# Layer B's projections of queries and keys: ScalarE reads a bank three times before VectorE's lower part

## The chip, the cores and the metric

The kernel runs on one core of one Trainium2 chip. The metric is device time in microseconds of one execution of the whole program (four layers). Five engines work in parallel, each through its own list of instructions in order: TensorE (PE, matrix products; PEld are its weight loads), VectorE (DVE), ScalarE (ACT), GpSimd (POOL) and SyncE (SP), which here issues most of the transfers. They wait for each other by semaphores. Matrix products land in PSUM, which the kernel uses as eight banks of 128 x 512 fp32 ("ps").

## The reference

Four layers run one after the other on a sequence of 2048 tokens of width 640, with 32 heads of width 20: A, B, A, B, each with a layer norm ahead and a residual sum behind.

```
x = x + A(layernorm(x)); x = x + B(layernorm(x)); x = x + A(...); x = x + B(...)

A: q, k, v = heads of x @ wqkv;  phi(t) = (t+1 if t > 0 else exp(t)) + 1e-6
   kv = sum_s phi(k) v^T;  z = sum_s phi(k)
   out = (phi(q) kv / (phi(q) z + 1e-6)) @ wo

B: q, k, v = x @ wq, x @ wk, x @ wv, cut into heads and 4 segments of 512 tokens
   phi(t) = t+1 if t > 0 else exp(t);  g = sigmoid(beta), one per head;  M = z = 0
   for each segment s:
       a_dot = softmax(q_s k_s^T / sqrt(20) + causal mask) v_s
       a_mem = phi(q_s) M / (phi(q_s) z + 1e-6)
       o_s   = g * a_mem + (1 - g) * a_dot
       M += phi(k_s) v_s^T;  z += sum phi(k_s)
   out = concat(o) @ wo
```

So the projected q and k of layer B are used twice: in the softmax attention of their own segment, and through phi in the memory. The first segment has no memory to read (M = 0), so its q needs no phi; the last has nobody to write a memory for, so its k needs none.

## The kernel before, in words

Numbers that need more than fp16 are carried as a sum of two fp16 tensors, an upper and a lower part. The weights and the normalized, transposed input are split like that, and a projection `proj_t` (L380 to L394) makes one bank of 128 output columns x 512 tokens from 15 matrix products of 512 columns (five blocks of 128 input columns, three products each).

Layer B's `b_project` (L867) handles a segment of 512 tokens: first v, then for each of the five blocks t of 128 columns q and then k. For each of these banks p:

- `split_store` (L853) takes the upper fp16 part with ScalarE (L857) and, from p and the upper part, the lower one with VectorE (L858), into a buffer `nat` (two of them). Then two transfers by SP's queue write both to memory, L861 and L862 for q, L864 and L865 for k.
- where phi is needed, `phi` (L419) makes e = exp(p) (L423) and r = relu(p) (L425) on ScalarE, both into a pool `er` of three buffers, and VectorE puts them together, min(e, 1) + r (L430), as `pq` for q or `pkT` for k. The bank is free when its last reader is done.

Of the 40 banks in one run of layer B, the 15 of q in segments 1 to 3 and the 15 of k in segments 0 to 2 have phi; the 5 of q in segment 0 and the 5 of k in segment 3 are split only. The layer runs twice, so 60 of 80 banks have phi. From pkT, TensorE makes a transpose (L885), ScalarE copies it (`pkt`, L887), and products with v (L893) are added to the memory `acc` by VectorE (L898, L900).

The attention of a segment (`attention`, L1106) starts when the segment's projections are done, and so runs beside the projections of the next segment. It works on 8 groups of four heads, in three stretches of steps each, with groups pipelined: row maxima (`row_max`: products L1008, VectorE's masked maximum L1015), the maxima as extra rows of q (`split_max` L1024, `max_rows`: transpose L1033, ScalarE's copy `mt` L1035, SP's transfer L1038), scores and exponentials (`scores`: products L1050, ScalarE's exponential `pe` L1054, GpSimd's causal mask L1061), the weighted sum with v (`weigh`, L1077), a copy (L1083), a transpose and the normalization (L1090 to L1101; `tmp` of L1100 comes from the pool `er` too). The stacks of q and k are loaded from memory by SP (L994).

Before that, layer A's end (`a_second`) and behind it the output projection of B (`b_out`) run as further streams; both transpose their input through a bank, which ScalarE (L329) and VectorE (L330) split into an upper and a lower part, called `oT`, for products at L401.

Two generators, one for the dense work and one for attention, are stepped by their estimated TensorE costs. TensorE's order is the order of the program text as these streams give it. The other engines' lists are ordered by the framework's scheduler from the dependencies, with the program order as priority. The framework also puts the wait for an earlier reader of a PSUM bank on another engine's next reader: in the kernel before, ScalarE's e waits for VectorE's lower part of the same bank.

Of the kernel before, what the change touches and what calls it, by code (L numbers as in the profile page):

```python
# [11 lines left out]
BF16 = mybir.dt.bfloat16  # L12
# [9 lines left out]
P = 128  # L22
C = D // P
SEG = 512
NSEG = S // SEG
# [102 lines left out]
def pause(n):  # L128
    for _ in range(n):
        yield 0.0  # L130
# [12 lines left out]
class Kernel:  # L143
# [272 lines left out]
        nc.vector.scalar_tensor_tensor(e, e, 1.0, r, op0=OP.min, op1=OP.add)  # L416
        return e

    def phi(self, p, inv, dst, eps):  # L419
        nc, sb = self.nc, self.sb  # L420
        n = p.shape[-1]
        e = sb.tile([P, 512], F32, tag="er", name="e", bufs=3)[:, :n]
        nc.scalar.activation(e, p, AF.Exp, scale=inv)  # L423
        r = sb.tile([P, 512], F32, tag="er", name="r", bufs=3)[:, :n]
        nc.scalar.activation(r, p, AF.Relu, scale=inv)  # L425
        if eps:
            nc.gpsimd.tensor_scalar(e, e, 1.0, eps, op0=OP.min, op1=OP.add)  # L427
            nc.vector.tensor_tensor(dst, e, r, op=OP.add)
        else:
            nc.vector.scalar_tensor_tensor(dst, e, 1.0, r, op0=OP.min, op1=OP.add)  # L430
# [419 lines left out]
            for a in (60, 124):  # L850
                nc.sync.dma_start(k[a:a + 2], one[:2])

    def split_store(self, p, dd, t, key):  # L853

        nc = self.nc
        nat = self.bp.tile([P, 2, SEG], F16, tag="nat", name="nat", bufs=2)
        nc.scalar.activation(nat[:, 0], p, AF.Copy, scale=QK_SHIFT)  # L857
        nc.vector.scalar_tensor_tensor(nat[:, 1], p, QK_SHIFT, nat[:, 0], op0=OP.mult, op1=OP.subtract)  # L858
        d = dd[t * P:(t + 1) * P]
        if key == "q":  # L860
            self.q_nat.dma_start(d[:, 0:3:2], nat)  # L861
            self.q_nat.dma_start(d[:, 1], nat[:, 0])  # L862
        else:
            self.q_nat.dma_start(d[:, 0:2], nat)  # L864
            self.q_nat.dma_start(d[:, 2], nat[:, 0])  # L865

    def b_project(self, st):  # L867

        nc, sb, bp = self.nc, self.sb, self.bp
        s, w, xT, acc = st["s"], st["w"], st["xT"], st["acc"]  # L870
        st["qd"] = self.dr.tile([D, 3, SEG], F16, tag="qd", name="qd", bufs=2)
        st["kd"] = self.dr.tile([D, 3, SEG], F16, tag="kd", name="kd", bufs=2)
        if "before" in st:
            yield lambda: st["before"].get("attended")
        for i in range(NT):
            st["v"].append(self.new_v(st))
            for n in range(2):
                self.v_half(self.proj_n(xT, w["v"], i, n), st["v"][i], n)
                yield self.COST_N
        pkT = pk = None  # L880

        def pk_turn():
            pt = self.bank()
            for i in range(NT):
                nc.tensor.transpose(pt[:, i * P:(i + 1) * P], pkT[:, i * P:(i + 1) * P], self.ident)  # L885
            pk = bp.tile([P, SEG], F32, tag="pkt", name="pkt", bufs=1)
            nc.scalar.activation(pk, pt, AF.Copy)  # L887
            return pk

        def update(t, pk):  # L890
            pm = self.bank()
            for i in range(NT):
                nc.tensor.matmul(pm[:, :WID[t]], pk[:, i * P:(i + 1) * P],  # L893
                                 st["v"][i][:, LO[t] * E1:LO[t] * E1 + WID[t]],
                                 start=i == 0, stop=i == NT - 1)
            a = acc[:, OFF[t]:OFF[t] + WID[t]]
            if s == 0:
                nc.vector.tensor_copy(a, pm[:, :WID[t]])  # L898
            else:
                nc.vector.tensor_tensor(a, pm[:, :WID[t]], a, op=OP.add)  # L900

        for t in range(C):
            p = yield from self.proj_t(xT, w["q"], t)
            self.split_store(p, st["qd"], t, "q")
            if s > 0:
                pq = sb.tile([P, SEG], F32, tag="pq", name="pq", bufs=PQ)
                self.phi(p, self.inv["B", "q"], pq, 0)
                st["pq"].append(pq)
            yield self.COST_T
            st["half"] = t >= 2  # L910
            if pkT is not None:
                pk = pk_turn()
                yield 440
            p = yield from self.proj_t(xT, w["k"], t)
            self.split_store(p, st["kd"], t, "k")
            if s < NSEG - 1:
                pkT = bp.tile([P, SEG], F32, tag="pkT", name="pkT", bufs=1)
                self.phi(p, self.inv["B", "k"], pkT, 0)
            yield self.COST_T
            if pk is not None:  # L920
                update(t - 1, pk)
                yield 4 * 4 * WID[t - 1] * COL
        st["projected"] = True

        def rest():
            if s == 0:
                yield from pause(4)
            if s < NSEG - 1:
                pk = pk_turn()
                yield 440  # L930
                update(C - 1, pk)
                yield 4 * 4 * WID[C - 1] * COL
                st["mem"] = self.masked(acc, self.gblk)
        st["rest"] = rest()
# [64 lines left out]
    def row_max(self, G, todo):  # L999

        nc, bp, qs, ks = self.nc, self.bp, G["qs"], G["ks"]
        bs = [self.bank() for _ in range(2)]
        cost = 0
        for p, i, a in todo:
            n = (i + 1) * P
            for par in range(2):
                r = slice(64 * par, 64 * par + 60)
                nc.tensor.matmul(bs[par][:, a:a + n], qs[r, p, i * P:(i + 1) * P], ks[r, p, :n],  # L1008
                                 start=True, stop=True)
                cost += n * COL  # L1010
        for par in range(2):
            for p, i, a in todo:
                n = (i + 1) * P
                junk = bp.tile([P, SEG], BF16, tag="junk", name="junk", bufs=1)
                nc.vector.tensor_tensor_reduce(bs[par][:, a:a + n], bs[par][:, a:a + n], self.maskw[:, SEG - n:],  # L1015
                                               1.0, NEG, OP.add, OP.max, G["mg"][:, par, p, i:i + 1])
        return cost
# [347 lines left out]
```

## Time and profile before

| | us |
|---|---|
| median of three runs | 1744.88 |
| lowest and highest | 1742.05, 1745.94 |
| the profiled execution | 1743.11 |
| its span in the trace | 1741.4 |

| engine | busy in the span |
|---|---|
| PE | 1668.7 us, 96% |
| DVE | 1183.8 us, 68% |
| PEld | 1048.4 us, 60% |
| ACT | 969.3 us, 56% |
| POOL | 518.7 us, 30% |

The mean granted TensorE clock of the execution is 0.998 of full speed. A line of the profile that names a group reads: source line, engine, operation, what it writes <- what it reads with shape and type, count, then busy time in us and mean ns of one, then the idle time of the engine ahead of these instructions and what ended most of it. A row of the timeline reads: start in us, duration, engine, line, operation, tiles, count of instructions joined in the row, and in brackets the engine's idle time just before with what released it. The chain that ended last is followed back from the last instruction, at each step to what released it.

### The profile page before, as it was taken

To read this page: it belongs to the slowest core of one execution; us is meant where nothing else is said; L and a number is where in the kernel's file an instruction comes from. 1 tells how busy PE (TensorE), PEld (TensorE's weight loads), DVE (VectorE), ACT (ScalarE), POOL (GpSimd) and SP (SyncE) were. 2 spreads that over 40 slices of the span, in tenths; PEclk is the share of its full clock that TensorE was granted. 3 is DMA by queue.
4 is the path that set the end of the run, shared out by engine and by line. 5 is a ranking of instruction groups with operands and counts; after the bars stand their busy time and mean duration, and the time that the engine had idled before them with its cause. 6 is when DMAs were issued, how large, how long until landed. Compare 5 with 4: busy or idle time off the path is not lost.

```text
span 1741.4 us, 36031 instructions
## 1 busy us (share of the span) xinstructions
PE 1668.7 (96%) x13032; PEld 1048.4 (60%) x13032; DVE 1183.8 (68%) x3856; ACT 969.3 (56%) x1818; POOL 518.7 (30%) x982
## 2 busy tenths in 40 slices
PE   6999999999999999999989999999999999999998
PEld 4676666654665566456556777666546545645555
DVE  8645534577787677758864466846778877878773
ACT  5545433357557646667665553333675576666674
POOL 1543350022123312333342311220422432333452
PEclk9999999999999999999999999999999999999999
DMA  7422453422322322352211303433232323223432
GB/s 264 181 109 95 155 188 105 136 70 81 118 69 70 113 93 81 124 191 67 78 43 39 114 31 122 159 105 124 66 105 83 112 80 106 102 81 111 137 108 92
DMA packets 118330, 187.59 MB, mean 108 GB/s; under 512 B 13948, under 2 KB 79612, under 8 KB 115848
## 3 DMA queue, kind: packets, MB, share of 16 engines
q1 hardware_dynamic: 105896, 142.68, 25.7%
q0 software_dynamic: 3040, 21.63, 3.4%
q10 hardware_dynamic: 9216, 20.98, 3.1%
q8 instruction: 103, 1.69, 0.4%
q14 instruction: 75, 0.61, 0.1%
HBM read 106.05 MB, written 78.64 MB: 106 GB/s over the span
## 4 chain that ended last, share of the span: by engine, by line
PE 77%; DVE 10%; ACT 6%; issue 2%; POOL 2%; DMA 2%; SPq 0%; ACTq 0%; POOLq 0%; DVEq 0%
PE ps L401 32%; PE ps L387 17%; PE ps L1077 8%; PE ps L1050 4%; PE ps L1008 3%; ACT pe L1054 3%; PE ps L325 3%; PE ps L566 3%; PE ps L456 3%; DVE ps L1015 2%; PE ps L1090 1%; PE ps L893 1%; PE ps L732 1%; DVE st L344 1%; DVE oT L330 1%
## 5 line engine op out<-in xcount | busy, mean ns | idle before, releaser
L1015 DVE CUSTOM_DVE_ANT_0 ps<-ps,maskw 128x512 f32<-128x512 f32 (+3 forms) x1024 | 472.8, 520 | 40.4 <-PE ps L1008 38.1
L1054 ACT ACTIVATE pe<-ps,lsc 128x512 f32<-128x512 f32 x640 | 395.0, 696 | 91.1 <-PE ps L1050 88.0
L1061 POOL TENSOR_SCALAR_AFFINE_SELECT pe<-pe 128x256 f32<-128x256 f32 (+1 forms) x640 | 230.1, 365 | 448.8 <-ACT pe L1054 434.9
L401 PEld LDWEIGHTS <-xT 128*128 128x128 f16 x2880 | 280.6, 98 | 114.8 <-issue 10.2
L401 PEld LDWEIGHTS <-oT 128*128 128x128 f16 x1920 | 186.1, 98 | 80.3 <-issue 6.5
L1077 PE MATMUL ps<-pe,v 128*32 128x512 f32 (+3 forms) x2048 | 161.4, 436 | 13.3 <-POOL pe L1061 6.9
L401 PE MATMUL ps<-w_Bo,oT 128*128 128x320 f16 x960 | 142.4, 301 | 2.5 <-ACT pe L1054 1.0
L1015 DVE DVE_READ_ACCUMULATOR2_ANT mg<- 128x1 f32 x1024 | 144.7, 141 | 0.0
L387 PE MATMUL ps<-xT,w_Bq 128*128 128x512 f16 x600 | 140.2, 379 | 1.9 <-ACT pe L1054 0.8
L401 PE MATMUL ps<-w_Bv,xT 128*128 128x320 f16 x960 | 139.7, 299 | 0.7 <-DVE otok L1097 0.6
L387 PE MATMUL ps<-xT,w_Bk 128*128 128x512 f16 x600 | 138.8, 379 | 1.2 <-ACT pe L1054 1.2
L401 PE MATMUL ps<-w_Ak,xT 128*128 128x320 f16 x960 | 136.1, 299 | 0.5 <-ACT r L415 0.5
L1008 PE MATMUL ps<-ks,qs 60*128 60x512 f16 (+3 forms) x1024 | 124.6, 297 | 8.9 <-ACT pe L1054 3.2
L858 DVE SCALAR_TENSOR_TENSOR nat<-ps,nat 128x512 f16<-128x512 f32 x80 | 55.2, 690 | 87.9 <-ACT nat L857 87.8
L1077 PEld LDWEIGHTS ps<-pe,v 128*32 128x32 f32 x2048 | 64.9, 109 | 73.4 <-issue 44.9
L1050 PE MATMUL ps<-qs,ks 62*128 62x512 f16 (+3 forms) x1024 | 105.7, 300 | 3.1 <-ACT pe L1054 1.1
L427 POOL TENSOR_SCALAR e<-e 128x320 f32<-128x320 f32 (+1 forms) x52 | 82.9, 1595 | 82.1 <-ACT e L423 77.9
L857 ACT ACTIVATE nat<-ps 128x512 f16<-128x512 f32 x80 | 48.2, 603 | 90.9 <-PE ps L387 71.6
L387 PEld LDWEIGHTS <-w_Bk 128*128 128x128 f16 x600 | 57.3, 98 | 65.4 <-issue 5.6
L387 PEld LDWEIGHTS <-w_Bq 128*128 128x128 f16 x600 | 56.7, 98 | 65.8 <-issue 7.8
L1008 PEld LDWEIGHTS <-qs 60*128 60x128 f16 x1024 | 50.3, 94 | 75.0 <-issue 47.7
L349 POOL TENSOR_TENSOR rs<-rs,mhalf 128x1 f32<-128x1 f32 x48 | 27.6, 576 | 218.7 <-DVE rs L348 218.7
(220 smaller groups left out, 2633.1 us busy)
## 6 DMA issues: line engine op xcount, KB each, us to landing
x<-xn ACTq DMA_DIRECT2D x48, 320.0 KB
qs<-qd SPq DMA_DIRECT2D x128, 120.0 KB
ks<-kd SPq DMA_DIRECT2D x128, 120.0 KB
xo<-x SPq DMA_DIRECT2D x48, 320.0 KB
pqi<-pqd SPq DMA_DIRECT2D x32, 320.0 KB
qd<-nat SPq DMA_DIRECT2D x40, 256.0 KB
kd<-nat SPq DMA_DIRECT2D x40, 256.0 KB
x<-in_A_x SPq DMA_DIRECT2D x16, 320.0 KB
```

Source lines behind the costliest of these rows:

```text
L325: nc.tensor.transpose(pt[:, (c - c0) * P:(c - c0 + 1) * P], src[:, c * P:(c + 1) * P], self.ident)
L387: nc.tensor.matmul(p, w[:, c, a, t * P:(t + 1) * P], xT[:, c, b, :], start=k == 0, stop=k == 3 * C - 1)
L401: nc.tensor.matmul(p, xT[:, c, a, i * P:(i + 1) * P], w[:, c, b, n * HN:(n + 1) * HN], start=k == 0, stop=k == 3 * C - 1)
L427: nc.gpsimd.tensor_scalar(e, e, 1.0, eps, op0=OP.min, op1=OP.add)
L456: nc.tensor.matmul(nd[:, lo - k * cut:hi - k * cut], pq[t], mem[:, OFF[t] + lo - a:OFF[t] + hi - a], start=first, stop=True, skip_group_ch ...
L858: nc.vector.scalar_tensor_tensor(nat[:, 1], p, QK_SHIFT, nat[:, 0], op0=OP.mult, op1=OP.subtract)
L1008: nc.tensor.matmul(bs[par][:, a:a + n], qs[r, p, i * P:(i + 1) * P], ks[r, p, :n], start=True, stop=True)
L1015: nc.vector.tensor_tensor_reduce(bs[par][:, a:a + n], bs[par][:, a:a + n], self.maskw[:, SEG - n:], 1.0, NEG, OP.add, OP.max, G["mg"][:, p ...
L1050: nc.tensor.matmul(b[:, a:a + n], ks[r, p, j * P:(j + 1) * P], qs[r, p, j * P:], start=True, stop=True)
L1054: nc.scalar.activation(e, b, AF.Exp, scale=self.lsc)
L1061: nc.gpsimd.affine_select(d, d, pattern=pat, compare_op=OP.is_ge, fill=0.0, base=0, channel_multiplier=-1)
L1077: nc.tensor.matmul(G["pv"][32 * h4:32 * h4 + 32, j * P:], v[j][:, h * E1:h * E1 + 32], G.pop((p, par, j)), start=j == 0, stop=j == 2, skip ...
```

## The change: what it does

`phi` is cut in two. A new helper `exp_relu` makes e and r, and `split_store` gets an argument that says whether phi is needed. If so, it calls `exp_relu` between the upper and the lower part and returns the pair, which `phi` then takes in place of making its own. So for the 60 banks with phi the program now has, in order: upper (ScalarE), e and r (ScalarE), lower (VectorE), the two stores, the sum (VectorE). Each instruction is the same as before in operands, shape and count. A tile `junk` in `row_max` that no instruction used is no longer allocated.

```diff
+    def exp_relu(self, p, inv):
         nc, sb = self.nc, self.sb
         n = p.shape[-1]
         e = sb.tile([P, 512], F32, tag="er", name="e", bufs=3)[:, :n]
         nc.scalar.activation(e, p, AF.Exp, scale=inv)
         r = sb.tile([P, 512], F32, tag="er", name="r", bufs=3)[:, :n]
         nc.scalar.activation(r, p, AF.Relu, scale=inv)
+        return e, r
+
+    def phi(self, p, inv, dst, eps, er=None):
+        nc = self.nc
+        e, r = er or self.exp_relu(p, inv)
...
-    def split_store(self, p, dd, t, key):
+    def split_store(self, p, dd, t, key, phi):
         nat = self.bp.tile([P, 2, SEG], F16, tag="nat", name="nat", bufs=2)
         nc.scalar.activation(nat[:, 0], p, AF.Copy, scale=QK_SHIFT)
+        er = self.exp_relu(p, self.inv["B", key]) if phi else None
         nc.vector.scalar_tensor_tensor(nat[:, 1], p, QK_SHIFT, nat[:, 0], op0=OP.mult, op1=OP.subtract)
...
+        return er
...
             p = yield from self.proj_t(xT, w["q"], t)
-            self.split_store(p, st["qd"], t, "q")
+            er = self.split_store(p, st["qd"], t, "q", s > 0)
             if s > 0:
                 pq = sb.tile([P, SEG], F32, tag="pq", name="pq", bufs=PQ)
-                self.phi(p, self.inv["B", "q"], pq, 0)
+                self.phi(p, self.inv["B", "q"], pq, 0, er)
...
             p = yield from self.proj_t(xT, w["k"], t)
-            self.split_store(p, st["kd"], t, "k")
+            er = self.split_store(p, st["kd"], t, "k", s < NSEG - 1)
             if s < NSEG - 1:
                 pkT = bp.tile([P, SEG], F32, tag="pkT", name="pkT", bufs=1)
-                self.phi(p, self.inv["B", "k"], pkT, 0)
+                self.phi(p, self.inv["B", "k"], pkT, 0, er)
...
-                junk = bp.tile([P, SEG], BF16, tag="junk", name="junk", bufs=1)
```

More of the change, by code (lines that the diff above doesn't have):

```diff
@@ L417, in phi_a @@
         return e
-    def phi(self, p, inv, dst, eps):
+    def exp_relu(self, p, inv):
         nc, sb = self.nc, self.sb
```

## The prediction

> **What bounds the kernel now.** I read the engine totals first, then the shares of the chain that ended last, then the costliest groups. On the page:
>
> ```profile
> span 1741.4 us, 36031 instructions
> PE 1668.7 (96%) x13032; PEld 1048.4 (60%) x13032; DVE 1183.8 (68%) x3856; ACT 969.3 (56%) x1818; POOL 518.7 (30%) x982
> PE 77%; DVE 10%; ACT 6%; issue 2%; POOL 2%; DMA 2%; SPq 0%; ACTq 0%; POOLq 0%; DVEq 0%
> L858 DVE SCALAR_TENSOR_TENSOR nat<-ps,nat 128x512 f16<-128x512 f32 x80 | 55.2, 690 | 87.9 <-ACT nat L857 87.8
> L857 ACT ACTIVATE nat<-ps 128x512 f16<-128x512 f32 x80 | 48.2, 603 | 90.9 <-PE ps L387 71.6
> ```
>
> TensorE is busy 96% of the span and carries 77% of the chain; VectorE and ScalarE have slack on average and matter where TensorE waits for a bank or an operand from them. The edited code runs in layer B's projections. Two stretches by time, columns start:end, length, then busy time and count of PE, PEld, DVE, ACT, POOL, clock, DMA share and rate:
>
> ```profile
> 395.00:470.00 75.00, 73.11 (x566) 39.18 (x567) 57.09 (x206) 54.18 (x96) 17.51 (x49) 1.00 0.30 95
> 1255.00:1330.00 75.00, 70.52 (x542) 35.40 (x540) 56.30 (x200) 52.87 (x96) 20.80 (x52) 1.00 0.28 89
> ```
>
> Here, where projections and attention are interleaved, TensorE is idle for only 1.9 and 4.5 of 75 us, at clock 1.00, so a delay of what it waits for shows and a gain can only come out of those idle spots.
>
> What the change attacks is in the waits by pair (total, times, longest) and the two ScalarE lines:
>
> ```profile
> ACT e L423 <- DVE nat L858: 23.3, 33, 1.0
> L423 ACT ACTIVATE e<-ps,inv_Bq x30: 667/687/784, 407.3 to 1590.3; 128x512 f32<-128x512 f32 x30
> L425 ACT ACTIVATE r<-ps,inv_Bq x30: 675/684/793, 407.8 to 1590.9; 128x512 f32<-128x512 f32 x30
> ```
>
> ScalarE sat idle 23.3 us, 33 times, because the exponential e had to wait until VectorE's lower part had read the same bank. The 60 banks that need the feature map (30 of q, 30 of k) have e and r; the other 20 of the 80 keep their order.
>
> **The change part by part.** Nothing is added or removed on any engine: TensorE's list is identical, and the dropped junk tile has no instruction, so both are costed at nothing. Per bank the chain before is upper (0.60), lower (0.69), e and r (by their starts, 1.27 together), then the sum pq or pkT on VectorE, off the bank. After it is upper, e, r, lower. A bank is held for about 0.60 + 1.27 + 0.69 either way, 2.6 us; one hand-over between the engines, some 0.06 us, goes. What changes is who is served meanwhile. In the changed program's lists ScalarE goes from "upper, attention exponentials, e, r" to "upper, e, r, attention exponentials"; on VectorE lower and sum become neighbours, and move behind the row maxima or the memory update, or ahead of an output transpose. In the program lower waits for ScalarE's r. The four effects that I find:
>
> *A. Attention exponentials now behind e and r.* One place, ScalarE, VectorE and TensorE in order of start:
>
> ```profile
> 1283.08 0.60 ACT L857 ACTIVATE nat<-ps 128x512 f16<-128x512 f32 x1 [2.96 <-PE ps L387]
> ...
> 1283.71 0.69 DVE L858 SCALAR_TENSOR_TENSOR nat<-ps,nat 128x512 f16<-128x512 f32 x1
> ...
> 1283.90 1.26 ACT L1054 ACTIVATE pe<-ps,lsc 128x512 f32<-128x512 f32 x2 [0.22 <-PE ps L1050]
> ...
> 1284.64 1.27 PE L893 MATMUL ps<-v,pkt 128*128 128x147 f32 x8 [0.40 <-ACT pe L1054]
> ...
> 1285.05 0.69 ACT L423 ACTIVATE e<-ps,inv_Bk 128x512 f32<-128x512 f32 x1
> ...
> 1285.62 0.70 ACT L425 ACTIVATE r<-ps,inv_Bk 128x512 f32<-128x512 f32 x1
> ```
>
> ```profile
> 575.72 2.20 PE L401 MATMUL ps<-w_Bo,oT 128*128 128x320 f16 x15 [0.40 <-ACT pe L1054]
> ...
> 1543.24 1.46 PE L387 MATMUL ps<-xT,w_Bk 128*128 128x512 f16 x6 [0.40 <-ACT pe L1054]
> ```
>
> TensorE already waits 0.40 us for the first exponential to free a bank. With e and r (1.27) ahead of it, and 0.22 of ScalarE's idle time filled, that exponential ends 1.27 − 0.22 = 1.05 us later. I find eight stalls of this form; the second fence shows the first and the last. Each is between 0 (a later stall of TensorE takes it up) and 1.27; I take 1.05, because the wait stands in the row and nothing lies between the exponential and TensorE: 8 × 1.05 = +8.4.
>
> *B. Output transposes now behind e, r, lower and sum.* Two banks, the q bank at 453 and this k bank:
>
> ```profile
> 591.37 0.61 ACT L857 ACTIVATE nat<-ps 128x512 f16<-128x512 f32 x1
> 591.84 0.41 ACT L329 ACTIVATE oT<-ps 128x256 f16<-128x256 f32 x1
> 592.01 0.69 DVE L858 SCALAR_TENSOR_TENSOR nat<-ps,nat 128x512 f16<-128x512 f32 x1 [0.22 <-ACT nat L857]
> 592.62 0.41 DVE L330 TENSOR_TENSOR oT<-ps,oT 128x256 f16<-128x256 f32 x1
> 592.74 0.69 ACT L423 ACTIVATE e<-ps,inv_Bk 128x512 f32<-128x512 f32 x1 [0.49 <-DVE nat L858]
> 593.09 0.38 PE L1008 MATMUL ps<-ks,qs 60*128 60x256 f16 x3 [0.40 <-DVE oT L330]
> 594.03 0.69 DVE L430 SCALAR_TENSOR_TENSOR pkT<-e,r 128x512 f32<-128x512 f32 x1
> ```
>
> ```profile
> 453.97 0.96 DVE L330 TENSOR_TENSOR oT<-ps,oT 128x384 f16<-128x384 f32 x2
> ...
> 454.98 2.32 PE L387 MATMUL ps<-xT,w_Bk 128*128 128x512 f16 x10
> ```
>
> TensorE waits for oT's subtraction at 593.09 and resumes with its end (453.97 + 0.96) at 454.98. After: upper ends at 591.98, e and r at about 593.25, lower at 594.0, sum at 594.7, oT at 595.1 against 593.03: up to 2.05 later. Lowest is 0, if the bank is not the next that TensorE wants; nearest is the wait in the row, so I take 1.9 for each: +3.8.
>
> *C. The start of attention after segment 0's projections,* where VectorE's row maxima are the chain:
>
> ```profile
> 336.68 0.69 DVE L858 SCALAR_TENSOR_TENSOR nat<-ps,nat 128x512 f16<-128x512 f32 x1 [2.98 <-ACT nat L857]
> ...
> 337.41 0.69 ACT L423 ACTIVATE e<-ps,inv_Bk 128x512 f32<-128x512 f32 x1 [0.76 <-DVE nat L858]
> ...
> 338.01 0.70 DVE L1015 CUSTOM_DVE_ANT_0 ps<-ps,maskw 128x512 f32<-128x512 f32 x1
> ...
> 338.79 0.63 DVE L430 SCALAR_TENSOR_TENSOR pkT<-e,r 128x512 f32<-128x512 f32 x1
> ```
>
> Before, lower ran in VectorE's idle time; after, r ends near 337.9 and lower falls among the maxima: between 0 and 0.69; as VectorE runs back to back from 338 on, I take 0.65. Once in each run of layer B: +1.3.
>
> *D. Gains.* Where ScalarE idled before e and TensorE then waits for what stands behind r:
>
> ```profile
> 412.33 0.69 ACT L423 ACTIVATE e<-ps,inv_Bk 128x512 f32<-128x512 f32 x1 [0.76 <-DVE nat L858]
> ...
> 413.48 2.42 ACT L1054 ACTIVATE pe<-ps,lsc 128x512 f32<-128x512 f32 x4
> ...
> 415.38 0.95 PE L1008 MATMUL ps<-ks,qs 60*128 60x512 f16 x5 [0.20 <-ACT pe L1054]
> ```
>
> ```profile
> 1327.11 0.69 ACT L1054 ACTIVATE pe<-ps,lsc 128x512 f32<-128x512 f32 x1 [0.79 <-PE ps L1050]
> ...
> 1330.06 0.63 PE L1077 MATMUL ps<-pe,v 128*32 128x256 f32 x6 [0.28 <-POOL pe L1061]
> ```
>
> At 413.48 the four exponentials move up by the 0.76, and the bank awaited at 415.38 with them: about 0.7. At 1330.06 the operand comes from an exponential behind r, and ScalarE's 0.79 idle is filled by e: about 0.75; the like at 1468.66 another 0.75. Two stalls for a bank that r frees (555.53 and 716.67) give about 0.25 each. Sum −2.7; at the least 0, at the most all 23.3 us of the wait. The rest of that idle time I count as nothing: TensorE has work meanwhile, 73.11 of 75 us in the first window; without that cover a bank gains up to 0.76.
>
> *Stores.* On SP the lower half's store of each of these 60 banks leaves 1.27 us later, and row loads queue behind it:
>
> ```profile
> SPq L861 <- DVE nat L858: 29.7, 30, 6.5
> SPq L1038 <- ACT mt L1035: 423.7, 61, 21.1
> ```
>
> SP spends 423.7 us waiting for row maxima to be ready, so a store that holds it 1.27 us longer mostly delays nothing. I take 0; the upper end is 1.27 per row load that is due at that moment.
>
> *Sum.* 8.4 + 3.8 + 1.3 − 2.7 = +10.8. TensorE holds 77% of the chain; for the rest I assume that a delay is taken up by another wait: 0.77 × 10.8 = +8.3. The profiled execution took 1743.11 us (1.7 around the span), so 1751.4; it lies 1.8 below the median of the three runs, 1744.88, by which it would be 1753.2. I give 1752.
>
> A rule bears on C and B. The Trainium skill, "PSUM — Partial Sum Buffer", section "PSUM bank collisions raise a hardware error", says that two engines' accesses to the same bank and partition quadrant must not coincide, two reads included, and that the compiler orders ScalarE against VectorE for it. The trace agrees for the order before (e waits for lower, 23.3 us); that lower will wait for r no run shows yet. Were it not so, lower would run beside e at its old place: C falls away and B shrinks to 2 × 1.3, the sum is 8.4 + 2.6 − 2.7 = 8.3, and 0.77 of it gives 1749.5.
>
> **The rivals.** *Faster, the other side:* ScalarE's idle time is what counts. By the timeline about 20 of the 33 waits lie in interleaved segments, at some 0.8 us like the rows under D: 16 us. If A's delays are taken up by TensorE's next stalls and a third of this reaches the chain, it is 1743.11 − 5.3 = 1737.8. For it: e's wait is real, and TensorE's gaps in the two windows, 1.9 and 4.5 us, are not used up by A's places alone. Against: TensorE's 0.40 waits at A's places are for the work that moves back. It decides if fewer than two of the eight stalls lengthen. The Trainium skill, "Perfetto Trace Analysis", section "Identifying the Most-Contended Engine", holds that busy time of matmuls is a poor measure of headroom and that of weight loads a better one; by it TensorE has room and this rival gains. This trace's clock of 1.00 and its chain of 77% speak for TensorE as the limit all the same.
>
> *Same:* every delay and gain is taken up within TensorE's next stall, as the bank's hold is unchanged to 0.06 us: 1743 to 1746. Against: the sites of A stand right on the chain.
>
> *Slower still:* the later stores hold SP where row loads are due. If six loads of a segment's groups are each held 1.27 us and TensorE waits: +7.6 more, 1759. Against: SP's slack above.
>
> **How the numbers follow.** 0.2%, 3.5 us, is about the least that a measurement of this kernel tells from no change; so faster is below 1741.4 and slower above 1748.4. Chances: my forecast 0.56, of which 0.04 falls short of the bound; slower still 0.14; same 0.10; faster 0.20. Together slower 0.66, same 0.14, faster 0.20. The likeliest case alone spans 1746 (half of A) to 1757 (no absorption, on the median). The range must hold most of the faster case and of the worse one: 1738 to 1760.
>
> **What would show it.** In the trace after: e's wait for lower gone, lower waiting for r instead; the PE rows at A's eight places with waits of about 1.4 instead of 0.40; oT's subtraction at 593 near 595; the waits at 415.38 and 1330.06 gone. I am wrong if A's waits stay near 0.4, or if they grow and TensorE's following stalls shrink by as much, or if new waits stand at the stores on SP.

## The result and the profile after

The changed kernel takes 1751.62 us (median of five, 1750.38 to 1753.72) against 1744.88 us: ratio 1.0041, 95% interval 1.003 to 1.0053. It is slower, by 6.7 us, and 1752 was predicted. The profiled execution took 1750.38 us. The page after, with the rows that answer to those of before:

```profile
span 1748.7 us, 36067 instructions
PE 1671.6 (96%) x13032; PEld 1046.7 (60%) x13032; DVE 1180.7 (68%) x3856; ACT 966.3 (55%) x1818; POOL 530.3 (30%) x982
...
PE 78%; DVE 8%; ACT 6%; POOL 2%; issue 2%; DMA 2%; SPq 1%; ACTq 0%; POOLq 0%; DVEq 0%
...
L864 DVE SCALAR_TENSOR_TENSOR nat<-ps,nat 128x512 f16<-128x512 f32 x80 | 55.2, 691 | 88.0 <-ACT r L425 53.1
```

The engines' counts are those of before, and so are the busy times within 3.1 us, but for GpSimd: 530.3 us instead of 518.7. The lower part (L864 now) waits for r. The waits by pair say the same:

```profile
DVE nat L864 <- ACT r L425: 53.1, 46, 3.7
...
DVE nat L864 <- ACT nat L862: 34.6, 16, 11.1
```

e's wait for the lower part, 23.3 us before, is gone from this view. The two windows with the same work as the two shown before:

```profile
395.79:474.36 78.57, 73.78 (x566) 38.87 (x567) 56.10 (x205) 54.10 (x96) 19.77 (x50) 1.00 0.27 85
1257.58:1334.07 76.49, 71.16 (x542) 35.21 (x540) 54.47 (x194) 52.49 (x96) 23.76 (x52) 1.00 0.27 86
```

Both are longer (75.00 before), TensorE's idle part grew (1.9 to 4.8 us, 4.5 to 5.3 us), and GpSimd is busier by 2 to 3 us with the same work (50 and 52 instructions, 49 and 52 before).

TensorE runs the same 13,032 products in the same order in both traces (six near 1228 us change places by their starts). So the start of each product after, less its start before, is the delay that has built up until there, and its steps tell where. At the last product it is 7.3 us. The steps of 0.4 us or more within layer B's projections (worked out from the two traces; steps within some 2 us of each other are joined; time of before, us; a product's line is its line before):

```
 415.38  -0.56  L1008   stall for an exponential gone
 418.08  +1.28  L1077   now waits for GpSimd's mask of pe
 426.31  -0.46  L387    wait for acc gone
 432.16  +1.38  L1077   now waits for the mask of pe
 440.81  +1.00  L893    now waits for the exponential
 454.25  +1.28  L1008   wait for pkt, now for the lower part
 555.53  -0.63  L1077   wait for a bank shorter (-0.28), -0.35 two us on
 593.09  +0.51  L401    now waits for the lower part
 716.67  -0.63  L1077   wait for a bank shorter (-0.28), -0.35 two us on
1263.80  +1.47  L1077   now waits for the mask of pe
1278.75  -0.71  L1077   wait for the mask shorter
1292.85  +1.47  L1077   now waits for the mask of pe
1309.88  -1.11  L1077   wait for the mask shorter
1318.62  +0.65  L387    now waits for the exponential
1330.06  -0.58  L1077   wait for the mask shorter
1426.56  +0.79  L387    now waits for the exponential
1468.66  -0.58  L1077   wait for the mask shorter
1565.68  +1.38  L1077   now waits for the mask of pe
1578.23  +1.47  L1077   now waits for the mask of pe
```

Six steps, 8.45 us together, stand at the weighted sum. One of them, in the timeline of before:

```profile
1291.04 1.29 ACT L1054 ACTIVATE pe<-ps,lsc 128x512 f32<-128x512 f32 x2
...
1291.82 0.41 POOL L1061 TENSOR_SCALAR_AFFINE_SELECT pe<-pe 128x256 f32<-128x256 f32 x1 [0.66 <-ACT pe L1054]
...
1291.93 1.56 PE L1077 MATMUL ps<-pe,v 128*32 128x384 f32 x24
1292.18 0.73 ACT L423 ACTIVATE e<-ps,inv_Bq 128x512 f32<-128x512 f32 x1
...
1292.40 0.41 POOL L1061 TENSOR_SCALAR_AFFINE_SELECT pe<-pe 128x256 f32<-128x256 f32 x1 [0.17 <-ACT pe L1054]
```

and the same place after:

```profile
1294.46 0.71 ACT L423 ACTIVATE e<-ps,inv_Bq 128x512 f32<-128x512 f32 x1
...
1295.03 0.72 ACT L425 ACTIVATE r<-ps,inv_Bq 128x512 f32<-128x512 f32 x1
...
1295.60 1.31 ACT L1060 ACTIVATE pe<-ps,lsc 128x512 f32<-128x512 f32 x2
...
1296.39 0.68 DVE L435 SCALAR_TENSOR_TENSOR pq<-e,r 128x512 f32<-128x512 f32 x1
1296.39 1.30 POOL L1067 TENSOR_SCALAR_AFFINE_SELECT pe<-pe 128x256 f32<-128x256 f32 x2 [1.81 <-ACT pe L1060]
...
1297.39 0.99 PE L1083 MATMUL ps<-pe,v 128*32 128x256 f32 x8 [0.96 <-POOL pe L1067]
```

Two things are to be seen. The two exponentials stand behind e and r and start 1.1 us later against the work around them. And the first of the two masks, which now begins in the same moment as VectorE's sum of e and r, takes 0.94 us, where before each took 0.41; the second, behind that sum, takes 0.40 (1.30 us for the two, as joined in the row).

### The profile page after: what moved, and what is told of

It reads as the page before. It is cut to its first block, busy times and chain, and to the rows that moved or that the text cites. A ratio compares the mean times of both kernels' runs of the same rounds, so it can differ in the third digit from the quotient of the medians.

```text
span 1748.7 us, 36067 instructions
## 1 busy us (share of the span) xinstructions
PE 1671.6 (96%) x13032; PEld 1046.7 (60%) x13032; DVE 1180.7 (68%) x3856; ACT 966.3 (55%) x1818; POOL 530.3 (30%) x982
## 4 chain that ended last, share of the span: by engine, by line
PE 78%; DVE 8%; ACT 6%; POOL 2%; issue 2%; DMA 2%; SPq 1%; ACTq 0%; POOLq 0%; DVEq 0%
PE ps L401 33%; PE ps L387 17%; PE ps L1083 7%; PE ps L1056 4%; PE ps L325 3%; PE ps L1015 3%; ACT pe L1060 3%; PE ps L461 3%; PE ps L571 3%; PE ps L900 1%; PE ps L1096 1%; DVE ps L1021 1%; PE ps L737 1%; ACT r L425 1%; PE ps L892 1%
## 5 line engine op out<-in xcount | busy, mean ns | idle before, releaser
L1021 DVE CUSTOM_DVE_ANT_0 ps<-ps,maskw 128x384 f32<-128x384 f32 (+3 forms) x1024 | 472.5, 519 | 47.0 <-PE ps L1015 42.7
L1067 POOL TENSOR_SCALAR_AFFINE_SELECT pe<-pe 128x256 f32<-128x256 f32 (+1 forms) x640 | 241.7, 386 | 417.1 <-ACT pe L1060 412.8
L864 DVE SCALAR_TENSOR_TENSOR nat<-ps,nat 128x512 f16<-128x512 f32 x80 | 55.2, 691 | 88.0 <-ACT r L425 53.1
```

Source lines behind the costliest of these rows:

```text
L1067: nc.gpsimd.affine_select(d, d, pattern=pat, compare_op=OP.is_ge, fill=0.0, base=0, channel_multiplier=-1)
```

## Experiments

To place the cost, `moved` decides bank by bank whether the new order applies; the 80 banks are numbered in program order, q and k in turn:

```diff
+    def moved(self, s, t, key):
+        n = (((len(self.jobs) - 1) * NSEG + s) * C + t) * 2 + (key == "k")
+        return CONDITION
...
-            er = self.split_store(p, st["qd"], t, "q", s > 0)
+            er = self.split_store(p, st["qd"], t, "q", s > 0 and self.moved(s, t, "q"))
```

and the same for k. Theory 1 is that an attention exponential behind e and r reaches GpSimd's mask late, and TensorE waits for it; theory 2 that a later lower part costs a little at every bank.

**Only the q banks.** CONDITION is `key == "q"`.

> Only the 30 q banks have e and r ahead of the lower part; the 30 k banks are as before. Theory 1 (the loss comes through the weighted sum: an attention exponential behind e and r reaches GpSimd's mask late, and TensorE waits for the masked operand): seven of the eleven stalls that grew belong to q banks, +9.2 us, and the shortened stalls of q banks give back 3 to 4, so about 1750.5. Theory 2 (the later lower part as such costs, evenly on all banks): half of the loss, about 1748.

Measured: 1755.27 us, ratio 1.0055 (1.0036 to 1.0073). All of the loss, and 5 us more than expected by theory 1; in its trace the last product is only 8.0 us late, as the profiled execution, 1751.17 us, was the shortest of the four (its granted clock was 0.999, that of the others 0.995 and 0.996). Why the q banks alone cost some 3 us more than q and k together was not followed up.

**Only the k banks.** CONDITION is `key == "k"`.

> Only the 30 k banks are changed. Theory 1: four stalls of k banks, +3.0 us, less about 1.7 from shortened ones: about 1746. Theory 2: half of the loss, about 1748.

Measured: 1744.61 us, ratio 1.0001 (0.9991 to 1.0011): no loss. The two runs together exclude theory 2, an even cost at every bank, since 30 banks with the lower part last cost nothing.

**All but the eleven banks at which a stall grew.** CONDITION:

```diff
+        return n not in (12, 14, 15, 16, 23, 50, 54, 57, 63, 74, 76)
```

> All changed but eleven banks, those at which a stall of TensorE grew by 0.5 us or more (together +12.2 us in the two traces), which keep the order of before. Theory 1: the loss goes and the shortened stalls stay, 1740 to 1743. Theory 2: 49 of 60 banks still changed, 49/60 of the loss, about 1750.5.

Measured: 1740.95 us, ratio 0.9974 (0.9964 to 0.9984). With 49 of the 60 banks in the new order the kernel is faster than the one before.

**The eleven alone.** `n in (...)` with the same list.

> Only the eleven banks of the grown stalls have the new order. Theory 1: the whole loss sits there; the changed kernel is 6.7 us above the one before and the kernel that spares the eleven 4.2 below, so these alone cost about 10.9: 1756. Rival (the eleven stall only because the other 49 banks have shifted the work): 1750 or less.

Measured: 1757.73 us, ratio 1.0078 (1.0061 to 1.0094), 13.0 us slower. The loss of the whole change, and more, sits in eleven banks, whatever the others do.

**Attention exponentials ahead, the lower part still last.** In `scores`:

```diff
-        nc.scalar.activation(e, b, AF.Exp, scale=self.lsc)
+        with self.tc.high_priority():
+            nc.scalar.activation(e, b, AF.Exp, scale=self.lsc)
```

> The changed kernel, with the attention exponentials of L1060 given priority over e and r on ScalarE; the lower part still comes after r. Theory 1 (the harm is exponentials behind e and r): the six stalls at the weighted sum, 7.9 us together, go, while oT and pkt may stand behind more than before: 1743 to 1747. Rival (the harm is the lower part in the last place, which frees the bank and fills VectorE late): 1750 or more.

Measured: 1740.78 us, ratio 0.998 (0.9971 to 0.999). The weighted sum at the same place, in this kernel's timeline:

```profile
1291.40 1.29 ACT L1061 ACTIVATE pe<-ps,lsc 128x512 f32<-128x512 f32 x2
...
1292.30 1.56 PE L1084 MATMUL ps<-pe,v 128*32 128x384 f32 x24
1292.55 0.73 ACT L423 ACTIVATE e<-ps,inv_Bq 128x512 f32<-128x512 f32 x1
...
1293.88 0.69 DVE L864 SCALAR_TENSOR_TENSOR nat<-ps,nat 128x512 f16<-128x512 f32 x1 [0.35 <-ACT r L425]
```

The lower part waits for r as in the changed kernel, but the exponentials are first, and TensorE runs its 24 products without a stall. All six steps at the weighted sum are gone in this trace (each changes by 0.1 us or less). This tells the order on ScalarE from the lower part's place: the harm is in the first.

**The control: the kernel before with that priority.**

> The kernel before with the same priority: the control for the run with the priority on the changed kernel. The order at the six weighted sums is the same as before, so within 2 us of 1745 by every theory; anything further off is the worth of the priority itself.

Measured: 1739.34 us, ratio 0.9966 (0.9953 to 0.9979): 5.4 us faster, where 2 at most were expected. So the priority has a worth of its own, and the run ahead of it does not show that the changed order is better than the old one. Against the changed kernel it removes 10.8 us, of which 5.4 are this worth, if the two add. In the trace it takes stalls away at weighted sums outside the projections too (2.4 us at 1371), and it lengthens some others, 2.35 us between 540 and 785.

**VectorE's sum ahead of the lower part.**

```diff
         er = None if phi is None else self.exp_relu(p, self.inv["B", key])
+        if phi is not None:
+            self.phi(p, self.inv["B", key], phi, 0, er)
         nc.vector.scalar_tensor_tensor(nat[:, 1], p, QK_SHIFT, nat[:, 0], op0=OP.mult, op1=OP.subtract)
```

with `phi` the destination pq or pkT.

> As the changed kernel, but VectorE makes the sum of e and r before the lower part. Theory 1a (GpSimd's masks take 0.83 instead of 0.41 us where they coincide with that sum, and six of the grown stalls contain some 0.35 us of this): the sum ends when the next exponential ends, the masks are back at 0.41, about 2 us less than the changed kernel, 1749.5. Rival: the overlap costs nothing on TensorE's path, and the bank is held 0.69 us longer: 1752 to 1755.

Measured: 1752.57 us, ratio 1.0043 (1.0031 to 1.0055): as slow as the changed kernel, so by the time it is the rival that came out. The trace shows more: nearly all the longer masks are gone, while other waits grew. GpSimd's masks, in the groups of before, after and of this kernel:

```profile
L1061 POOL TENSOR_SCALAR_AFFINE_SELECT pe<-pe 128x256 f32<-128x256 f32 (+1 forms) x640 | 230.1, 365 | 448.8 <-ACT pe L1054 434.9
```

```profile
L1067 POOL TENSOR_SCALAR_AFFINE_SELECT pe<-pe 128x256 f32<-128x256 f32 (+1 forms) x640 | 241.7, 386 | 417.1 <-ACT pe L1060 412.8
```

```profile
L1068 POOL TENSOR_SCALAR_AFFINE_SELECT pe<-pe 128x256 f32<-128x256 f32 (+1 forms) x640 | 231.1, 367 | 427.6 <-ACT pe L1061 424.3
```

and the timeline of this kernel at the weighted sum shown above:

```profile
1296.81 0.69 DVE L435 SCALAR_TENSOR_TENSOR pq<-e,r 128x512 f32<-128x512 f32 x1 [0.23 <-ACT r L425]
1297.42 0.68 DVE L866 SCALAR_TENSOR_TENSOR nat<-ps,nat 128x512 f16<-128x512 f32 x1
1297.42 0.41 POOL L1068 TENSOR_SCALAR_AFFINE_SELECT pe<-pe 128x256 f32<-128x256 f32 x1 [1.81 <-ACT pe L1061]
...
1297.88 1.21 PE L1084 MATMUL ps<-pe,v 128*32 128x256 f32 x8 [0.43 <-POOL pe L1068]
```

Beside the lower part, which reads one operand from PSUM, the mask takes 0.41, and the masks in sum are 10.6 us shorter than in the changed kernel. The six steps shrink from between 1.28 and 1.47 us to between 1.0 and 1.2, by 0.1 to 0.3 each, 1.7 us together. More than this was lost at one place that the theory did not see, 3.4 us at 1450 (time of before): GpSimd began an operation on `pqi` only 6.1 us after SP had issued the load of `pqi` (3.6 us in the changed kernel's trace), VectorE waited 2.65 us for it, and an output transpose queued behind. VectorE's list has the same order there as in the changed kernel. Why that load came late, and whether it does in every execution, one trace does not show.

```profile
1454.70 1.46 PE L387 MATMUL ps<-xT,w_Bq 128*128 128x512 f16 x6
...
1455.77 1.54 POOL L778 TENSOR_TENSOR pqi<-pqi,zb 128x640 f32<-128x640 f32 x1 [4.20 <-DMA pqi<-pqd]
...
1457.35 0.82 DVE L781 TENSOR_REDUCE rca<-pqi 128x32 f32<-128x640 f32 x1 [2.65 <-POOL pqi L778]
...
1458.77 0.38 PE L1016 MATMUL ps<-ks,qs 60*128 60x384 f16 x3 [1.47 <-DVE oT L330]
...
1460.63 1.91 PE L387 MATMUL ps<-xT,w_Bk 128*128 128x512 f16 x4
```

**Fourteen spared.** The tuple of eleven with 9, 49 and 51 added.

> As the kernel that spares eleven banks, with three more spared: the last k bank of segment 0 in both runs of the layer (stalls grown by 0.46 and 0.44 us) and the first k bank of segment 1 in the second (grown by 0.41). Theory 1: 1.3 us less, 1739.6; if these three stalls were passed on to later ones, the same as with eleven, 1741.

Measured: 1739.74 us, ratio 0.9969 (0.9958 to 0.9981). 1.2 us below the run with eleven, as expected, but within the intervals of both.

**Only the eight banks at which a stall got shorter.** `n in (11, 13, 20, 30, 52, 56, 59, 69)`.

> The mirror of the run with the eleven alone: only the eight banks at which a stall of TensorE got shorter by 0.46 to 1.11 us when they were changed without the eleven (5.2 us together) have the new order. If gains are local like the losses: 1744.7 - 5.2 = 1739.5. If two of them, the shortened waits for the masked operand, are only what earlier losses left over: 1.8 less gain, 1741.5.

Measured: 1741.66 us, ratio 0.9977 (0.9967 to 0.9986), 4.1 us faster. Against the kernel before in the same session (1745.73) the gain lies midway between the two expected, 5.2 and 3.2, so it is not settled whether all eight gains are local.

**Both measures, each where it gains.** First the fourteen spared banks and the priority of the exponentials in the second run of layer B only; then, in that second run, the old order for all banks.

```diff
-        nc.scalar.activation(e, b, AF.Exp, scale=self.lsc)
+        second = len(self.jobs) > 1 and any(G["st"] is x for x in self.jobs[1])
+        with self.tc.high_priority() if second else nullcontext():
+            nc.scalar.activation(e, b, AF.Exp, scale=self.lsc)
```

> The kernel that spares fourteen banks, with the attention exponentials given priority in the second run of layer B, where the trace of the kernel before with that priority had gained 8 us after 1190 us (and lost 4 before). If both gains add: 1739.7 - 5 = about 1735; if both take the same idle time of ScalarE: 1738 to 1740.

> The new order only in the first run of layer B (with its spared banks), the order of before with the priority of the attention exponentials in the second. From the windows of the traces: 3.5 to 4 us gained in the first run, 7 in the second: 1735.

Measured: 1737.35 us, ratio 0.9954 (0.994 to 0.9969), and 1734.92 us, ratio 0.9947 (0.9931 to 0.9964). The second, with the condition `n < 40` added to the fourteen, is by its median the fastest kernel here, some 10 us under the one before and 16 to 17 under the changed one; with four executions of each, the intervals of the two overlap. The first gained 8.4 us against the kernel before in the same session, between the 9.7 of both gains added and the 4.7 to 6.7 of both taking the same idle time of ScalarE, so which holds is not settled.

## Why the prediction was right, point by point

The sign and the size came out, and so did the mechanism behind the main term, exponentials that come later behind e and r; the places where TensorE pays for it did not. By the signs that the prediction itself had set, e's wait is gone, the lower part waits for r, oT's subtraction comes late at 593 and the waits at 415.38 and 1330.06 are gone; but waits of about 1.4 us at A's eight places did not appear, and so A's account of them was wrong.

*A, exponentials behind e and r, +8.4.* The mechanism holds, by the runs with the eleven alone and with the exponentials first. The step that failed is "nothing lies between the exponential and TensorE" at the eight stalls for a bank. The place shown before, after:

```profile
1286.72 0.60 ACT L862 ACTIVATE nat<-ps 128x512 f16<-128x512 f32 x1 [2.96 <-PE ps L387]
...
1287.21 0.68 ACT L423 ACTIVATE e<-ps,inv_Bk 128x512 f32<-128x512 f32 x1
...
1287.45 0.49 DVE L1103 TENSOR_TENSOR otok<-ps,rc 128x320 f32<-128x320 f32 x1
...
1287.78 0.69 ACT L425 ACTIVATE r<-ps,inv_Bk 128x512 f32<-128x512 f32 x1
1288.08 1.24 PE L900 MATMUL ps<-v,pkt 128*128 128x147 f32 x8 [0.21 <-DVE otok L1103]
1288.35 1.85 ACT L1060 ACTIVATE pe<-ps,lsc 128x512 f32<-128x512 f32 x3
```

The exponential is indeed later, but TensorE waits for another reader: the bank it gets is the one that the normalization has freed, whose product with the reciprocal now runs ahead of the lower part. The framework deals the banks out when it builds the program: in the two built programs 251 of 2369 tiles follow another tile in their bank. So all eight waits got shorter, by 0.13 to 0.28 us, instead of 1.05 longer; with what stands beside two of them these places changed by −0.8 us together instead of +8.4. The delay came in by the other consumer of the same exponentials, the masked operand of the weighted sum: six steps, +8.45, and three products that wait for an exponential at k banks, +2.4. That the six steps nearly agree with A's +8.4 is luck: too much at one consumer, nothing at the other. Of the +8.45, the longer masks make 1.7, by the run with the sum first; the prediction did not have this cost.

*B, output transposes, +3.8.* Right place, half the size, +1.8 (of which 0.44 at 454 is a wait for an exponential just behind):

```profile
457.73 0.69 DVE L864 SCALAR_TENSOR_TENSOR nat<-ps,nat 128x512 f16<-128x512 f32 x1 [1.80 <-ACT r L425]
...
458.47 0.52 PE L1015 MATMUL ps<-ks,qs 60*128 60x256 f16 x4 [1.24 <-DVE nat L864]
...
596.28 0.43 ACT L329 ACTIVATE oT<-ps 128x256 f16<-128x256 f32 x1
...
597.21 1.52 PE L401 MATMUL ps<-w_Bo,oT 128*128 128x320 f16 x10 [1.10 <-DVE nat L864]
...
597.67 0.42 DVE L330 TENSOR_TENSOR oT<-ps,oT 128x256 f16<-128x256 f32 x1
```

TensorE waits for the lower part itself, not for the transpose behind it: again another bank was next. The transpose came at 597.67, 1.75 us late against the 3.3 us by which the work around it was already shifted, near the forecast 2.05; but no product waited for it.

*C, the start of attention, +1.3.* Less than forecast. At 339 TensorE lost 0.46, at 1198 it gained 0.17. In the second run the cost appeared only 30 us on, 0.6 net between 1190 and 1250; with bank 49 spared, as in the run with fourteen, that stretch is as before.

*D, gains, −2.7.* Measured −0.56, −0.58 and −0.58, and −0.28 at each of the two waits for a bank (0.39 us left of 0.67): −2.3, each at its forecast place and within 0.2 us. A further −0.35 came two microseconds behind each of the two banks.

*Stores, 0.* SP waits longer for the lower part, little at the stores of q (29.7 us before) but ten times as long at those of k (4.2 before); its slack remained (406.7 us before the row transfers):

```profile
SPq L1044 <- ACT mt L1041: 406.7, 54, 21.0
...
SPq L870 <- DVE nat L864: 41.1, 36, 1.6
...
SPq L867 <- DVE nat L864: 37.5, 36, 3.7
```

None of the steps above stands at a row transfer. The one wait of TensorE for such a transfer that grew, at 707.67, grew by 0.29 us, so the slower rival did not come about.

*The factor 0.77.* The steps add up to the 7.3 us at the last product as they stand, with the gains among them, so nothing shows a discount of this kind. The factor brought the raw sum of 10.8 to 8.3, nearer to the 6.7 measured, for another reason: B had 2.0 us too much, the gains at 426, 1278 and 1309, −2.3, were missing, and A, with the k banks' products counted, had 1.7 too little. That these nearly balance is luck as well.

*The rival "faster"* had the size of its gain about right: 4 to 5 us remain when eleven or fourteen banks keep the old order, near its 5.3. It was to win if fewer than two of the eight stalls lengthened. None did, and yet the kernel got slower, because eleven other waits grew: the condition watched the wrong places. The Trainium skill's rule, "PSUM — Partial Sum Buffer", section "PSUM bank collisions raise a hardware error", that accesses of two engines to one bank and quadrant are kept apart, reads included, agrees with the traces in both orders: e waited for the lower part, 23.3 us, and now the lower part waits for r, 53.1 us.

## What to carry to other kernels

When a shared engine's list is reordered, price the delay at every consumer of what is pushed back, the operand as well as the bank, by asking for each product which of its inputs comes last; which bank is freed last is itself dealt anew by the change. Apply such an order where the moved work meets idle time and not where an operand of TensorE waits in the queue: here 11 of 60 banks carried 13 us of loss, and the rest gained 4. And compare two traces product by product where the order on the bounding engine is the same; the steps show the places that totals by line hide.

## What was not expected of the hardware

*A mask of GpSimd takes twice as long beside a VectorE sum of two SBUF tensors.* Beside the row maxima or alone it mostly took 0.29 (128x128) or 0.41 us (128x256). The sum of e and r was the main work beside it once in the trace of before (0.53 us) and for 30 masks of the changed kernel, with medians of 0.88 (pkT) and 0.83 us (pq). With the sum first it was the main work beside six masks only (median 0.50), and the others were back at 0.29 or 0.41. The Trainium skill, "SBUF — State Buffer", section "Who interferes with whom", says that a VectorE instruction with two inputs in SBUF contends with a GpSimd instruction that reads SBUF, and that one with at most one, outside the modes that use two ports, does not; both halves agree with these rows (0.83 beside the sum, 0.41 beside the lower part).

*TensorE at half rate for a few microseconds.* In the timeline rows of the run with the sum first, six 512-column products took 1.46 us before the stall of 1.47 us, and four took 1.91 us behind it. The windows of the two places in that kernel, with the granted clock (0.50 and 1.00) as the third number from the end:

```profile
1460.60:1463.00 2.40, 2.40 (x8) 0.91 (x6) 2.40 (x10) 0.60 (x1) 2.05 (x5) 0.50 0.22 75
1454.70:1456.50 1.80, 1.80 (x12) 0.99 (x9) 0.00 (x1) 0.68 (x2) 0.73 (x1) 1.00 0.78 225
```

The clock was 0.50 there, and cost 1.3 us beyond the stalls. By the clock that the traces record, each trace has one to four such stretches while products run, of 3.41 us each (in two traces one is 6.83), not all at the same places from run to run. The changed kernel has one at 1233, in the stretch of C, where it slows ten products, 1.3 us together; this went into a wait that shrank from 1.48 to 0.49 us. The times of single executions go with the clock: of the 23 executions of the kernel before beside the run with the q banks, the three with a mean clock of 0.999 took 1740.16 to 1743.97 us, and the one with 0.994 took 1749.34. So two traces can differ by a microsecond or more for this reason alone. What starts a stretch was not tried.
